# Later transform ends for two batches, the older path for their first tiles, and packed tiles moved to the last four batches

## The chip, the cores and the metric

The kernel runs on one NeuronCore of a Trainium2 chip. The metric is the device time of one execution in microseconds (us), the median of the runs shown. The engines are named as in the profile: PE (TensorE matmuls), PEld (its weight loads), DVE (VectorE), ACT (ScalarE), POOL (GpSimd) and SP (SyncE, which here only issues DMAs).

## The reference, cut to what matters

There are 8 batches of 3008 positions by 256 channels. Each is filtered along the sequence in the frequency domain, and then every position goes through a two-layer network ("MLP") with a sigmoid-gelu between the layers.

```
X = np.fft.rfft(x, axis=1)
y = np.fft.irfft(X * (filt_r + 1j * filt_i)[None], n=3008, axis=1)     # y: (8, 3008, 256)
h = y.reshape(-1, 256) @ w_in                                           # (24064, 2048)
out = (h * (1 / (1 + np.exp(-1.702 * h)))) @ w_out                      # (24064, 256)
```

## The kernel before, in words

**The MLP.** Each batch is cut into 6 tiles `(b, t)`, 48 in all. A tile has 512 positions; the last tile of an even batch has 384. A tile takes 16 chunks `fc` of 128 hidden features. Values are split into a high and a low fp32r part, so one chunk is 12 matmuls: 6 in `first` (L854, into `h`), gelu twice on ACT (L858 and L859), the low part on DVE (L860, `gl`), and 6 in `second` (L879, into `o`). In program order `first` runs two chunks ahead of `second`.

**The transform.** `fft(b)` makes batch b's transform as a prime-factor transform of 64 by 47 points in two stages. It is a generator, and so one "leg" of the plan. For b > 1 the first stage is `packed()` with 24 half steps (butterfly on POOL L524, split L530 and L531, `transform` on PE L542 and then ACT and DVE L544 to L546, result to the DRAM tensor `a_d`). The second stage, `two()`, has 16 rounds. In each, `forward(i)` loads `a_d` (on POOL's queue) and the filter (`load_f`, on SP's queue), transforms (L609, `s`), merges two half results (L628, L629), multiplies by the filter (L631 to L639) and splits the product into `zy` (L643, L644). `backward(i)` transforms back (L609, `i`), merges (L617, L618) and writes `b_d` in DRAM. Batch b's leg runs under the MLP of batch b - 1, and its first stage overlaps the end of the leg before.

**The tiles' last step.** A tile's MLP input `y` is made from `b_d` by one of three paths. `signal`: load `br` (SP), for each half m four fp32 matmuls of 128 columns (L719), a copy on ACT (L727) and a difference on DVE (L728). `turned_signal` with `turned_passes`: load `br`, split on ACT and POOL (L795, L796), 3 matmuls of 512 columns for each half (L308 to L310), a transpose on DVE (L804), a store to the DRAM tensor `z_d`, four loads back, and a split on ACT and POOL (L736, L737). `turned_signal` with `packed_passes` is a variant with 4 matmuls (L769) in place of 6, and with more work on ACT, DVE and POOL (L759, L760, L770, L771, L774, L824). `is_packed` chooses between the last two.

**What sets the order.** The whole program is unrolled. A loop over the "turns" n (one for each chunk; batch b's first tile starts at n = 96 b) emits the MLP, and beside it what falls due: `due` holds for each tile the turns, counted from the chunk 16 before its start, at which its path takes a step, and `steps` holds the legs' steps by a planned time in units of a quarter chunk. `upto` is the planned end of a leg, and `SPACED` places the first stage ahead of the end of the leg before it. The framework's scheduler then orders each engine's instructions by its own estimate, but instructions marked `keep_in_program_order` keep their order among each other on their engine: on PE all matmuls of the legs, the first of each three in `turned_passes`, and the first L719 of `signal` when t is 0. Buffers that matter are the 7 `raw` ones, and the PSUM rings "f" and "h".

Of the kernel before, what the change touches and what calls it, by code (L numbers as in the profile page):

```python
# [14 lines left out]
ALU = mybir.AluOpType  # L15

B, S, D, DFF = 8, 3008, 256, 2048
# [4 lines left out]
Q = 112  # L22
NFC = DFF // P
# [8 lines left out]
def _tables():  # L32
# [66 lines left out]
    e_0 = de[:, 2:4, rows].reshape(P, 2, 2, 2, NH).transpose(0, 1, 4, 3, 2)  # L99
    sign = np.zeros((P, NS))  # L100
    sign[0:48] = sign[64:Q] = _places()[3]
    t1 = t1.reshape(P, 2, 2, NS // 2, 2).transpose(0, 1, 3, 2, 4)
    t1_s = t1[:N1].reshape(N1, 2, P // 2)
# [11 lines left out]
def _places():  # L115

    n1, q = np.arange(N1), np.arange(NH)
    n2 = np.stack([NH - 1 - q, NH + q])  # L120
    at = (N2 * n1[None, :, None] + N1 * n2[:, None, :]) % S
    time = np.where(n2[:, None, :] < N2, at, S)
    p, s = np.arange(48)[:, None], np.arange(NS)[None, :]
    k1 = np.where(s == 0, np.where(p < 24, 0, 32), s)
    k2 = np.where(s == 0, p % 24, p)
    freq = (k1 * N2 * pow(N2, -1, N1) + k2 * N1 * pow(N1, -1, N2)) % S
    sign = np.where(freq > S // 2, -1.0, 1.0)
    freq = np.where(freq > S // 2, S - freq, freq)
    freq = np.where((p < 47) | (s == 0), freq, S // 2 + 1)
    token, odd = [], None  # L130
    for b in range(B):
        for t in range(6):
            if b > 2 or b and t:
                blocks = (b * S + time[:, :, 4 * t : 4 * t + 4]).reshape(4, 32, 4).transpose(0, 2, 1)
                parts = [a.ravel() for a in blocks]
                if t == 5:
                    parts[2:] = parts[2][:96], parts[3][:96]
                    if b % 2:
                        parts[3:] = odd[:32], parts[3], odd[32:]
                    else:  # L140
                        parts[3], odd = parts[3][:32], parts[3][32:]
                token += parts
                continue
            for i in range(4):
                block = b * S + time[:, :, 4 * t + i]
                if 4 * t + i < NH - 1:
                    token.append(block.ravel())
                else:
                    odd = block[0]
    return time, freq, np.concatenate(token), sign  # L150


def _layout(a):

    x, fr, fi, wi, wo = a
    time, freq = _places()[0:2]
    x = np.concatenate([x, np.zeros((B, 1, D), x.dtype)], 1)[:, time]
    x0 = x[:2].reshape(2, P, 6, 4, D).transpose(0, 2, 1, 3, 4)
    x = x[2:].reshape(B - 2, 2, N1, 6, 2, 2, D).transpose(0, 3, 4, 2, 1, 5, 6)
    x = np.concatenate([x0, x.reshape(B - 2, 6, P, 4, D)])  # L160
    f = np.stack([fr, fi], 1)
    f = np.concatenate([f, np.zeros((1, 2, D), f.dtype)])[freq]
    f = f.reshape(48, NS // 2, 2, 2, D).transpose(1, 0, 2, 3, 4)
    f = np.concatenate([f, np.zeros((NS // 2, 16, 2, 2, D), f.dtype)] * 2, 1)
    wi = wi.reshape(2, P, NFC // 2, D).transpose(2, 1, 0, 3)
    wo = wo.reshape(NFC // 2, 2, P, D).transpose(0, 2, 1, 3)
    return {"x": x, "filt": f, "w_in": wi, "w_out": wo}
# [3 lines left out]
def tile_kernel(  # L171
# [9 lines left out]
    nc = tc.nc  # L181
# [38 lines left out]
    table, at = {}, 0  # L220
# [242 lines left out]
    def fft(b):  # L463
# [128 lines left out]
        def load(i):  # L592
            for k in range(2):
                src = a_d[k, 4 * i : 4 * i + 4].rearrange("q n d -> n q d")
                nc.gpsimd.dma_start(zy[0][64 * k : 64 * k + 48, i % 2].rearrange("p k s d -> p (k s) d"), src)  # L595

        def load_f(i):
            for k in range(2):
                load_in(f_buf[64 * k : 64 * k + 48, 2 * (i % 2) : 2 * (i % 2) + 2], fs[i])

        def second(i, m, src, name, k):

            pin = tc.keep_in_program_order
            ps = ring("f", [P, 2, D], f"{name}_{b}_{i}_{k}")
            if i == 0:
                pin(nc.tensor.matmul(ps[:, 0], de_sb[:, k, m + 1], src[:, k, 0], start=True, stop=True))
                nc.tensor.matmul(ps[:, 1], de_sb[:, k, m], src[:, k, 1], start=True, stop=True)
            else:
                pin(nc.tensor.matmul(ps, de_sb[:, k, m], src[:, k], start=True, stop=True))  # L609
            return ps  # L610

        def sides(k):
            return slice(64 * k, 64 * k + 48), slice(64 - 64 * k, 112 - 64 * k)
# [6 lines left out]
        def forward(i):  # L620

            u1, u2 = c_buf[i % 3], u_buf[i % 2]
            fr = f_buf[:Q, 2 * (i % 2) : 2 * (i % 2) + 2]
            f_r, f_i = fr[:, :, 0, :], fr[:, :, 1, :]
            for k in range(2):
                h, o = sides(k)
                ps = second(i, 0, zy[0][:, i % 2], "s2", k)
                nc.scalar.copy(u1[h], ps[o])  # L628
                nc.vector.tensor_tensor(ps[h], ps[h], u1[h], ALU.add)  # L629
                if k:  # L630
                    nc.vector.scalar_tensor_tensor(u2[o], ps[h], -1.0, f_i[h], ALU.mult, ALU.mult)  # L631
                else:
                    nc.vector.tensor_tensor(u2[o], ps[h], f_i[h], ALU.mult)
                nc.vector.tensor_tensor(u1[h], ps[h], f_r[h], ALU.mult)  # L634
                if k == 0:
                    yield
            if i + 2 < 16:
                load(i + 2)
            nc.gpsimd.tensor_tensor(u1, u1, u2, ALU.add)  # L639
            y = zy[0][:, 2 + i % 2]  # L640
            for k in range(2):
                h, o = sides(k)
                nc.scalar.copy(y[h, k], u1[h])  # L643
                nc.gpsimd.tensor_tensor(y[o, k], u1[h], y[h, k].bitcast(F32), ALU.subtract)  # L644
            if i + 2 < 16:
                load_f(i + 2)
            yield
# [18 lines left out]
        return slice(64 * k, 64 * k + 64)  # L666

    def is_packed(b, t):
        return 1 < t < 5 and b > 1 or b == B - 1 and t > 0

    def signal(b, t, y):

# [236 lines left out]
    ys, t2_two, gelu, s1_pool, t2_w, begin = {}, [], [], [], [], []  # L909

    def start(b, t):
        ys[b, t] = sb.tile([P, 2, 2, 512], F32R, tag="y", name=f"y_{b}_{t}")
        return (turned_signal if b > 2 or b and t else signal)(b, t, ys[b, t])

    tus.append(const.tile([P, 4, 2, 2, D], F32, tag="zy", name="w_tu"))
    conv = conversion()
    run(first_fft())
    load_unit(EARLY + 7)
    run(start(0, 0))
    run(conv, 3)  # L920
    load_unit(EARLY + 8)
# [17 lines left out]
    LEAD = 16  # L939

    def width(i):
        return 4 if tiles[i][1] < 5 or tiles[i][0] % 2 else 3

    due = {}
    for j in range(2, len(tiles)):
        b, t = tiles[j]
        if j == 2:
            steps = 23, 26, 27
        else:
            if is_packed(b, t):  # L950
                at = (-8, -4, -3, -2, -1, 0, 1, 2, 4, 8, 9, 10)
            else:
                at = (-6, -2, -1, 0, 1, 3, 9, 10) if b and t else (1, 3, 9) if t else (-1, 2, 3, 4, 5, 7, 11, 12) if b > 2 else (8, 11, 12) if b > 1 else (9, 12, 13)
            steps = [NFC * (j - 1) + k for k in at]
        for n in steps:
            due.setdefault(n, []).append(j)
    steps, passed, since = [], 0, 0
    for b in range(1, B):
        upto = sum(NFC * width(i) for i in range(6 * b)) - 4 * LEAD - ((18 if b > 2 else 12) * width(6 * b - 1) if b > 1 else 26)
        if b == 1:  # L960
            at = np.cumsum(FIRST_LEG) * (upto / sum(FIRST_LEG))
            one, two = at[:12], at[12:]
        else:
            early, beside, alone = SPACED[min(b, 4) - 2]
            first = since - 4 * early
            last = since + 4 * alone
            if not early:
                since = first = first + 4 * 5.5
            lead = first - 4 * np.array([5.0, 4.0, 2.2, 1.1])
            one = [*lead, *(first + (since - first) * np.arange(beside) / max(beside, 1))]  # L970
            one += list(since + (last - since) * (np.arange(24 - beside) / (23 - beside)))
            two = [last + 4 * 1.5, last + 4 * 3, *(last + 4 * 4 + (upto - last - 4 * 4) * np.cumsum([0.0, *LATER[1:]]) / sum(LATER[1:]))]
        one = [*one, two[0]]
        steps += [(when, b, which) for which, ats in enumerate((one, two)) for when in ats]
        since = upto
    steps.sort()
    legs = {}
    for n, (i, fc) in enumerate(turns):
        b, t = tiles[i]
        if n == 0:  # L980
            run(start(*tiles[1]))
# [61 lines left out]
```

## Time and profile before

| | us |
|---|---|
| median of 3 runs (2348.61 to 2349.15) | 2348.69 |
| the profiled execution | 2346.19 |
| its span, first to last instruction | 2344.4 |
| PE busy in it | 2323.5 (99%) |
| DVE, ACT, POOL busy | 1582.4 (67%), 1644.5 (70%), 1191.3 (51%) |

The span is the time from the first to the last instruction of one execution that the hardware profiler took. "Busy" is the time in which an engine had an instruction at work; for PE the ends of matmuls are modelled, so the share alone does not say how near PE is to its best.

### The profile page before, as it was taken

To read this page: it belongs to the slowest core of one execution; us is meant where nothing else is said; L and a number is where in the kernel's file an instruction comes from. 1 tells how busy PE (TensorE), PEld (TensorE's weight loads), DVE (VectorE), ACT (ScalarE), POOL (GpSimd) and SP (SyncE) were. 2 spreads that over 40 slices of the span, in tenths; PEclk is the share of its full clock that TensorE was granted. 3 is DMA by queue.
4 is the path that set the end of the run, shared out by engine and by line. 5 is a ranking of instruction groups with operands and counts; after the bars stand their busy time and mean duration, and the time that the engine had idled before them with its cause. 6 is when DMAs were issued, how large, how long until landed. Compare 5 with 4: busy or idle time off the path is not lost.

```text
span 2344.4 us, 32513 instructions
## 1 busy us (share of the span) xinstructions
PE 2323.5 (99%) x10590; PEld 1937.6 (83%) x10590; DVE 1582.4 (67%) x2374; ACT 1644.5 (70%) x3000; POOL 1191.3 (51%) x1079
## 2 busy tenths in 40 slices
PE   9999999999999999999999999999999999999999
PEld 7878888888888878788888888988888888888887
DVE  7978767677767767577776777667777767533332
ACT  6667768678777767677776777767877777655553
POOL 3035547457556665556655567545764465322220
PEclk9999999999999999999999999999999999999999
DMA  9274545666556565566557575656655565321200
GB/s 338 81 197 104 125 92 160 144 140 144 128 151 130 131 139 151 131 132 130 142 150 151 115 142 136 164 127 140 127 126 151 135 144 110 88 61 48 87 28 19
DMA packets 200120, 301.32 MB, mean 129 GB/s; under 512 B 19216, under 2 KB 136080, under 8 KB 199952
## 3 DMA queue, kind: packets, MB, share of 16 engines
q1 hardware_dynamic: 123248, 188.76, 28.8%
q0 software_dynamic: 46592, 44.05, 13.1%
q10 hardware_dynamic: 30112, 66.44, 11.0%
q8 instruction: 85, 1.39, 0.3%
q14 instruction: 83, 0.68, 0.1%
HBM read 184.35 MB, written 114.82 MB: 128 GB/s over the span
## 4 chain that ended last, share of the span: by engine, by line
PE 62%; DMA 1%; ACT 0%; POOL 0%; issue 0%; DVE 0%; SPq 0%; ACTq 0%; POOLq 0%; DVEq 0%
PE h L854 29%; PE o L879 28%; PE i L609 1%; PE s L609 1%; PE s L542 1%; PE i L769 1%; DMA br<-b_d 0%; PE i L308 0%; PE i L310 0%; PE i L309 0%; DMA z_d<-zt 0%; DMA s_pool<-in_x_dram 0%; SPq L211 0%; DMA a_d<-s_pool 0%; POOL y L737 0%
## 5 line engine op out<-in xcount | busy, mean ns | idle before, releaser
L854 PE MATMUL h<-y,wi 128*128 128x512 f32 (+1 forms) x4608 | 1180.6, 386 | 8.1 <-ACT y L736 3.0
L854 PEld LDWEIGHTS h<-y,wi 128*128 128x128 f32 x4608 | 861.0, 188 | 178.1 <-DVE gl L860 6.3
L860 DVE TENSOR_TENSOR gl<-h,gh 128x512 fp32r<-128x512 f32 (+1 forms) x768 | 518.4, 677 | 528.9 <-ACT h L859 474.3
L879 PE MATMUL o<-gh,wo 128*128 128x512 f32 (+1 forms) x3072 | 836.9, 385 | 0.8 <-ACT gh L858 0.8
L858 ACT ACTIVATE gh<-h 128x512 fp32r<-128x512 f32 (+1 forms) x768 | 452.6, 589 | 419.2 <-PE h L854 345.3
L879 PEld LDWEIGHTS o<-gh,wo 128*128 128x128 f32 x3072 | 573.5, 188 | 111.8 <-ACT gh L858 1.7
L879 PE MATMUL o<-gl,wo 128*128 128x512 f32 (+1 forms) x1536 | 485.4, 385 | 0.4 <-DVE gl L860 0.4
L859 ACT ACTIVATE h<-h 128x512 f32<-128x512 f32 (+1 forms) x768 | 449.3, 585 | 0.1
L879 PEld LDWEIGHTS o<-gl,wo 128*128 128x128 f32 x1536 | 287.3, 188 | 56.4 <-DVE gl L860 1.5
L644 POOL TENSOR_TENSOR zy<-c_buf,zy 48x512 fp32r<-48x512 f32 x224 | 288.5, 1288 | 82.9 <-ACT zy L643 71.3
L639 POOL TENSOR_TENSOR c_buf<-c_buf,u_buf 112x512 f32<-112x512 f32 x112 | 144.7, 1292 | 203.8 <-DVE c_buf L634 202.4
L595 POOL DMA_DIRECT2D zy<-a_d x224 | 130.1, 586 | 220.9 <-PE s L609 126.5
L531 POOL TENSOR_TENSOR e<-s_pool,e 64x512 fp32r<-64x512 f32 x144 | 185.4, 1287 | 50.9 <-ACT e L530 27.9
L618 DVE TENSOR_TENSOR b<-i,b 48x512 f32<-48x512 f32 x224 | 153.7, 686 | 71.6 <-ACT b L617 68.6
L629 DVE TENSOR_TENSOR s<-s,c_buf 48x512 f32<-48x512 f32 x224 | 156.9, 700 | 41.8 <-ACT c_buf L628 35.9
L643 ACT CAST zy<-c_buf 48x512 fp32r<-48x512 f32 x224 | 138.4, 618 | 45.7 <-POOL c_buf L639 39.1
L617 ACT COPY b<-i 48x512 f32<-48x512 f32 x224 | 130.0, 580 | 52.0 <-PE i L609 41.0
L634 DVE TENSOR_TENSOR c_buf<-s,f_buf 48x512 f32<-48x512 f32 x224 | 154.2, 689 | 3.0
L628 ACT COPY c_buf<-s 48x512 f32<-48x512 f32 x224 | 130.1, 581 | 25.0 <-PE s L609 18.3
L524 POOL TENSOR_TENSOR s_pool<-s_pool 128x512 f32<-128x512 f32 x72 | 93.0, 1292 | 82.4 <-DMA s_pool<-in_x_dram 64.8
L545 DVE TENSOR_TENSOR s_pool<-s,s_pool 64x512 f32<-64x512 f32 x144 | 98.8, 686 | 36.2 <-ACT s_pool L544 33.8
L760 POOL TENSOR_TENSOR z<-br,z 64x512 fp32r<-64x512 f32 x80 | 101.7, 1295 | 23.9 <-issue 21.0
(135 smaller groups left out, 1879.3 us busy)
## 6 DMA issues: line engine op xcount, KB each, us to landing
f_buf<-fs SPq DMA_DIRECT2D x224, 192.0 KB, 3.0
zy<-a_d POOLq DMA_DIRECT2D x224, 192.0 KB, 4.0
a_d<-s_pool ACTq DMA_DIRECT2D x144, 256.0 KB, 3.3
br<-b_d SPq DMA_DIRECT2D x124, 256.0 KB, 5.3
out_dram<-out SPq DMA_DIRECT2D x43, 512.0 KB, 3.4
b_d<-b ACTq DMA_DIRECT2D x112, 192.0 KB, 2.5
z_d<-zt SPq DMA_DIRECT2D x40, 512.0 KB, 2.7
s_pool<-in_x_dram SPq DMA_DIRECT2D x36, 512.0 KB, 4.2
```

The source lines that it names most:

```text
L531: nc.gpsimd.tensor_tensor(es[n, h][o], src[t], es[n, h][t].bitcast(F32), ALU.subtract)
L618: nc.vector.tensor_tensor(dst[h], ps[h], dst[h], ALU.add)
L629: nc.vector.tensor_tensor(ps[h], ps[h], u1[h], ALU.add)
L634: nc.vector.tensor_tensor(u1[h], ps[h], f_r[h], ALU.mult)
L639: nc.gpsimd.tensor_tensor(u1, u1, u2, ALU.add)
L643: nc.scalar.copy(y[h, k], u1[h])
L644: nc.gpsimd.tensor_tensor(y[o, k], u1[h], y[h, k].bitcast(F32), ALU.subtract)
L854: ins = nc.tensor.matmul(ps[:, :w], wi_sb[half][:, wk, kc, c], y[:, yk, kc, :w], start=n == 0, stop=n == 5)
L858: nc.scalar.activation(gh[:, :w], ps[:, :w], AF.Gelu_apprx_sigmoid)
L859: gelu.append(nc.scalar.activation(ps[:, :w], ps[:, :w], AF.Gelu_apprx_sigmoid).ins)
L860: nc.vector.tensor_tensor(gl[:, :w], ps[:, :w], gh[:, :w].bitcast(F32), ALU.subtract)
L879: ins = nc.tensor.matmul(pos[m][:, :w], wb[:, P * m : P * m + P], g[:, :w], start=first_one, stop=last_one)
```

## The change

The planned ends of the transforms of batches 3 and 4 (the fourth and the fifth, counted from 0) move from 18 chunks before the batch's first tile to 12 and to 14. The first tiles of these two batches take the path `signal` and its due turns (8, 11, 12) in place of `turned_signal` and (-1, 2, 3, 4, 5, 7, 11, 12); the order of the output positions follows. `is_packed` held for tiles 2 to 4 of batches 2 to 7 and for tiles 1 and 5 of batch 7; now it holds for tiles 1 to 5 of batches 4 to 7. In `forward`, for batch 1 only, the sum of the two halves goes to `u1` in SBUF instead of back into PSUM, the product with `f_r` is one DVE instruction for both halves, and the copies into `zy` run on DVE in place of ACT.

```diff
@@ -130,7 +130,7 @@
     token, odd = [], None
     for b in range(B):
         for t in range(6):
-            if b > 2 or b and t:
+            if b > 4 or b and t:
                 blocks = (b * S + time[:, :, 4 * t : 4 * t + 4]).reshape(4, 32, 4).transpose(0, 2, 1)
                 parts = [a.ravel() for a in blocks]
                 if t == 5:
@@ -626,12 +626,16 @@
                 h, o = sides(k)
                 ps = second(i, 0, zy[0][:, i % 2], "s2", k)
                 nc.scalar.copy(u1[h], ps[o])
-                nc.vector.tensor_tensor(ps[h], ps[h], u1[h], ALU.add)
+                total = ps if b > 1 else u1
+                nc.vector.tensor_tensor(total[h], ps[h], u1[h], ALU.add)
                 if k:
-                    nc.vector.scalar_tensor_tensor(u2[o], ps[h], -1.0, f_i[h], ALU.mult, ALU.mult)
+                    nc.vector.scalar_tensor_tensor(u2[o], total[h], -1.0, f_i[h], ALU.mult, ALU.mult)
                 else:
-                    nc.vector.tensor_tensor(u2[o], ps[h], f_i[h], ALU.mult)
-                nc.vector.tensor_tensor(u1[h], ps[h], f_r[h], ALU.mult)
+                    nc.vector.tensor_tensor(u2[o], total[h], f_i[h], ALU.mult)
+                if b > 1:
+                    nc.vector.tensor_tensor(u1[h], ps[h], f_r[h], ALU.mult)
+                elif k:
+                    nc.vector.tensor_tensor(u1, u1[:Q], f_r, ALU.mult)
                 if k == 0:
                     yield
             if i + 2 < 16:
@@ -640,7 +644,7 @@
             y = zy[0][:, 2 + i % 2]
             for k in range(2):
                 h, o = sides(k)
-                nc.scalar.copy(y[h, k], u1[h])
+                (nc.scalar.copy if b > 1 else nc.vector.tensor_copy)(y[h, k], u1[h])
                 nc.gpsimd.tensor_tensor(y[o, k], u1[h], y[h, k].bitcast(F32), ALU.subtract)
             if i + 2 < 16:
                 load_f(i + 2)
@@ -666,7 +670,7 @@
         return slice(64 * k, 64 * k + 64)
 
     def is_packed(b, t):
-        return 1 < t < 5 and b > 1 or b == B - 1 and t > 0
+        return t > 0 and b > 3
 
     def signal(b, t, y):
 
@@ -910,7 +914,7 @@
 
     def start(b, t):
         ys[b, t] = sb.tile([P, 2, 2, 512], F32R, tag="y", name=f"y_{b}_{t}")
-        return (turned_signal if b > 2 or b and t else signal)(b, t, ys[b, t])
+        return (turned_signal if b > 4 or b and t else signal)(b, t, ys[b, t])
 
     tus.append(const.tile([P, 4, 2, 2, D], F32, tag="zy", name="w_tu"))
     conv = conversion()
@@ -950,13 +954,13 @@
             if is_packed(b, t):
                 at = (-8, -4, -3, -2, -1, 0, 1, 2, 4, 8, 9, 10)
             else:
-                at = (-6, -2, -1, 0, 1, 3, 9, 10) if b and t else (1, 3, 9) if t else (-1, 2, 3, 4, 5, 7, 11, 12) if b > 2 else (8, 11, 12) if b > 1 else (9, 12, 13)
+                at = (-6, -2, -1, 0, 1, 3, 9, 10) if b and t else (1, 3, 9) if t else (-1, 2, 3, 4, 5, 7, 11, 12) if b > 4 else (8, 11, 12) if b > 1 else (9, 12, 13)
             steps = [NFC * (j - 1) + k for k in at]
         for n in steps:
             due.setdefault(n, []).append(j)
     steps, passed, since = [], 0, 0
     for b in range(1, B):
-        upto = sum(NFC * width(i) for i in range(6 * b)) - 4 * LEAD - ((18 if b > 2 else 12) * width(6 * b - 1) if b > 1 else 26)
+        upto = sum(NFC * width(i) for i in range(6 * b)) - 4 * LEAD - ((18 if b > 4 else 14 if b > 3 else 12) * width(6 * b - 1) if b > 1 else 26)
         if b == 1:
             at = np.cumsum(FIRST_LEG) * (upto / sum(FIRST_LEG))
             one, two = at[:12], at[12:]
```

## Rows read from the trace of the kernel before

**Rows 1.** Waits of PE, whole span: us in total, times, longest

```profile
PE h L854 <- ACT y L736: 3.0, 1, 3.0
PE h L854 <- DVE gl L860: 2.8, 4, 1.4
PE s L542 <- DVE s_pool L546: 2.3, 2, 1.4
PE h L854 <- POOL y L737: 2.1, 2, 1.8
PE i L609 <- DVE b L618: 1.9, 2, 1.7
```

**Rows 2.** Windows: length, busy us (instructions) by engine, clock, DMA

```profile
354.40:647.00 292.60, 292.60 (x1305) 242.85 (x1304) 213.75 (x316) 219.06 (x390) 181.11 (x162) 1.00 0.61 144
825.00:852.00 27.00, 24.47 (x104) 19.01 (x103) 15.36 (x24) 18.02 (x32) 16.73 (x16) 1.00 0.70 126
930.00:939.00 9.00, 3.65 (x15) 2.12 (x14) 7.94 (x13) 3.99 (x8) 2.65 (x3) 0.88 0.80 238
...
1180.00:1235.00 55.00, 54.27 (x239) 44.20 (x237) 39.31 (x58) 39.94 (x71) 31.96 (x26) 1.00 0.59 163
...
60.00:157.00 97.00, 96.32 (x438) 78.96 (x437) 88.51 (x150) 63.85 (x119) 20.39 (x13) 1.00 0.40 122
157.00:354.40 197.40, 194.45 (x943) 165.64 (x942) 141.53 (x217) 137.95 (x256) 91.72 (x89) 1.00 0.53 118
```

**Rows 3.** Timeline at batch 3's first tile: start, us, instruction [idle before]

```profile
930.97 2.96 SPq L211 DMA_DIRECT2D y<-z_d  x4
...
938.32 0.62 ACT L736 CAST y<-y 128x512 fp32r<-128x512 f32 x1 [2.55 <-DMA y<-z_d]
...
942.41 5.90 PE L854 MATMUL h<-y,wi 128*128 128x512 f32 x15 [1.77 <-POOL y L737]
```

**Rows 4.** Timeline before 850 us, SP's queue and ACT

```profile
824.15 13.09 SPq L211 DMA_DIRECT2D f_buf<-fs  x2
...
845.75 0.62 ACT L795 CAST bh<-br 128x512 fp32r<-128x512 f32 x1 [1.69 <-DMA br<-b_d]
```

**Rows 5.** Timeline of `signal` at batch 2: its loads, its matmuls

```profile
626.09 2.62 SPq L211 DMA_DIRECT2D br<-b_d  x4
...
641.67 1.05 PE L719 MATMUL i<-tab,br 128*128 128x128 f32 x8
642.48 0.48 PE L854 MATMUL h<-y,wi 128*128 128x512 f32 x1
```

**Rows 6.** L854 alone, windows from a leg's last L609 to the next batch

```profile
621.00:646.90 25.90, 11.56 (x42) 7.89 (x42) 1.00 0.68 179
903.55:938.98 35.43, 12.70 (x60) 10.69 (x60) 0.97 0.67 185
1190.05:1229.90 39.85, 19.42 (x73) 13.67 (x73) 1.00 0.64 177
1473.85:1509.20 35.35, 17.00 (x86) 15.07 (x85) 1.00 0.69 191
```

**Rows 7.** Timeline of POOL at batch 5's first tile

```profile
1508.16 2.54 POOL L737 TENSOR_TENSOR y<-y 128x512 fp32r<-128x512 f32 x2
```

**Rows 8.** Groups by line: xcount, busy us, mean ns, idle before

```profile
L634 DVE TENSOR_TENSOR c_buf<-s,f_buf 48x512 f32<-48x512 f32 x224 | 154.2, 689 | 3.0
...
L643 ACT CAST zy<-c_buf 48x512 fp32r<-48x512 f32 x224 | 138.4, 618 | 45.7 <-POOL c_buf L639 39.1 <-DVE gl L860 2.1 <-DVE b L618 0.7
...
L274 DVE TENSOR_SCALAR w_tu<-w_tu 128x512 uint32<-128x512 uint32 x16 | 6.7, 421 | 0.1
...
L770 ACT COPY uv<-i 64x512 f32<-64x512 f32 x80 | 46.5, 581 | 20.4 <-PE i L769 18.6
...
L760 POOL TENSOR_TENSOR z<-br,z 64x512 fp32r<-64x512 f32 x80 | 101.7, 1295 | 23.9 <-issue 21.0 <-ACT z L759 0.8
...
L281 DVE TENSOR_TENSOR w_tu<-w_tu 128x512 f32<-128x512 f32 x16 | 14.0, 874 | 0.4
```

## The prediction

> **What bounds the kernel now.** I read the page first (PE busy 99% of the span), then the chain of waits, which is PE almost throughout, and so asked only two things: how fast PE goes when nothing stops it, and where it is stopped. In the long window of batch 1, PE issues 1305 matmuls in 292.60 us without idle, 0.224 us each [rows 2]. The waits of PE show how little there is to win elsewhere: the five largest entries sum to 12.1 us [rows 1]. They are not spread out. Placing them by windows, 9.00 - 3.65 = 5.35 us lie between 930 and 939 us [rows 2], and another 1.77 us just after [rows 3]: batch 3's first tile starts late. Two smaller holes are 27.00 - 24.47 = 2.53 us around 847 us and 55.00 - 54.27 = 0.73 us around batch 4's first tile [rows 2].
>
> At batch 3's first tile the chain is plain [rows 3]: SP issues the four loads back from `z_d` over 930.97 to 933.93, ACT's L736 waits for them until 938.32, POOL's L737 follows, and PE's first weights wait for both. After this idle time the next 15 matmuls take 5.90 us, 0.393 each: the granted clock is down to the lower of its two levels (1.2 instead of 2.4 GHz), which cost 5.90 - 15 x 0.224 = 2.5 us. The late start costs 5.35 + 1.77 + 2.5 = 9.6 us in all.
>
> At 847 us an SP instruction is at fault [rows 4]: SP stands on filter loads from 824.15 for 13.09 us, tile 17's `br` load queues behind them, ACT's L795 waits 1.69 us for it with batch 3's L617 behind, and PE's L609 waits 1.7 us for L618 [rows 1].
>
> **How late the legs end.** The plan can be compared with the trace by counting L854 between a leg's last L609 and the next batch's first tile [rows 6]: x42, x60, x73, x86, so 7, 10, 12 and 14 chunks for batches 2 to 5. Working out from `steps` at which turn that L609 is planned, with PE's program three chunks ahead of it, gives 11, 17, 18 and 17. The legs lag by 4, 7, 6 and 3 chunks. From first to last L609 step, the plan gives second stages of 60, 66, 69 and 75 chunks; batch 3's is short, runs beside three packed tiles, and lags most. What the paths need: `turned_signal` at batch 5 takes from 1473.85 [rows 6] to the end of L737 at 1508.16 + 2.54 [rows 7], 36.9 us, and PE just doesn't wait. `signal` at batch 2 has its loads issued by 628.7, 7.7 us after the last L609 [rows 5, 6]. With 4.4 us to land (933.93 to 938.32, the nearest row [rows 3]), 0.81 us of L719 (641.67 to 642.48 [rows 5]), 0.58 + 0.69 us for copy and difference (like L770 and L634 [rows 8]) and some 0.8 us for the second half, it needs 15 us.
>
> **The change part by part.**
>
> *First tiles of batches 3 and 4.* Removed are, for each, a `z_d` store, four loads back on SP, two splits on ACT and POOL before and after, and two transposes. PE: 6 x 0.224 = 1.35 us become 0.81 us, so 2 x 0.54 = 1.1 us are saved for certain. In return the first L719, whose place in PE's order is kept, can stop PE with the MLP behind it, if `br` is late. Batch 3's last L609 is now planned 12 chunks ahead. With a lag of 4 to 7, 5 to 8 chunks of 2.5 to 3.0 us are left, 12 to 24 us against a need of 15. The stall of 9.6 us goes, and 0 to 2.5 us come back; I take 1, since tiles 14 to 16 are no longer packed and the second stage has 71 chunks, so less lag than 7 is due. Batch 4 has 14 - 6 = 8 chunks of 3 us, 24 us: its 0.7 us goes.
>
> *Packing moved.* Six tiles leave (batches 2 and 3), six come (tiles 1 and 5 of batches 4 to 6): PE keeps its 20 packed tiles and gains nothing. A packed tile costs ACT two more casts and four copies, 2 x 0.62 + 4 x 0.58 = 3.6 us, DVE four adds, 2.8 us, and POOL four more instructions of 1.3 us, 5.2 us [rows 8], and two more loads on SP. Under batch 2, where the filter loads block SP, it lifts this load: the 2.5 us at 847 us go (0 to 2.5; I take all, because SP's block begins behind the late rounds of batch 3). It is laid on batches 4 to 6. Batch 5's leg also loses four chunks at its start (75 to 71), so its lag should come near the 6 of batch 4: 1 to 3 chunks of 35.35 / 14.3 = 2.47 us later, against slack that may be as much as 4 us (POOL's L737 stands behind other work there) or none. This is 0 to 7.4 us of new idle at 1509 us, and up to 10 with the clock; I take 2.5.
>
> *Batch 1's `forward`.* ACT loses 32 copies of 0.62 us, 19.8 us. DVE loses two products of 0.69 us a round and gets one, over all partitions but with the same elements each, and two copies from SBUF, not shown in the trace: between 0.42 (L274, one SBUF source) and 0.69 us (a product) [rows 8]. Over 16 rounds DVE gains 16 x (0.15 to 0.69) = 2.4 to 11 us in a window where it is busy 141.53 of 197.40 us and PE idles 2.95 [rows 2]. From 60 to 157 us DVE is busy 88.51 of 97.00 and PE idles 0.68: at 91% it still serves PE. So this is free, 0 with bounds of -2.9 (all idle gone) and +3; the freed PSUM bank helps only where PE waits for one.
>
> DVE's sums and products would now read two SBUF operands (or copy within SBUF) while POOL works in SBUF too. The only such case to price is L281 at 0.874 us against 0.689 for L634 [rows 8]: 0.19 us for each of 16 x 5 instructions, 15 us of DVE, still 85% busy. By the Trainium skill, page "SBUF — State Buffer", section "SBUF: two separate sides", DVE instructions with two SBUF inputs or in a two-port mode and POOL exclude each other for the whole instruction. By that rule the longer L281 is such a wait, and the sum would be rival 4 below instead of 0.
>
> **Sum.** -9.6 - 2.5 - 0.7 - 1.1 + 1.0 + 2.5 = -10.4 us. The profiled execution took 2346.19 (span 2344.4 and 1.8 around it), 2.5 below the median of the runs, 2348.69. So 2335.8 there, and 2338 for the median.
>
> **Rivals.**
>
> 1. *No give-back.* Neither batch 3 nor batch 5 stalls: 2348.7 - 13.9 = 2335; with batch 1's idle gone too, 2332. Against it: batch 5 has no visible slack.
> 2. *The stall moves to batch 5.* Its lag becomes 6 or 7, like batch 3's, with a 384-wide tile ahead of it as there, so 9 to 10 us come back instead of 2.5: 2345. The denser leg and the packed tile 29 speak for it, its 14 chunks against batch 3's 10 against it.
> 3. *The move does nothing at batch 3.* The lag grows with the later end to 9 and more, 3 chunks or 8 us are left of the 15 needed, and 7 us of idle and 2.5 of slow clock stay: 2338 + 8.5 = 2346. Batch 2's leg, denser yet without packed tiles, lags by only 4.
> 4. *Slower, by DVE in batch 1.* Each of the 80 instructions waits for half a POOL instruction of 1.3 us: 52 us, DVE comes to 141.5 + 11 + 52 = 204 us in 197, and PE waits for `gl`. It decides from 91% on (180 us); the 24 us above go to PE: 2362. Against it: only 0.19 us a piece is seen.
>
> **How the numbers follow.** About 0.2%, 4.7 us, is what a measurement of this kernel can tell from no change. Forecast 0.48 (2334 to 2343); rivals 1: 0.14, 2: 0.20, 3: 0.10, 4: 0.08. Below 2344.0 lie the forecast, rival 1, half of rival 2 and a third of rival 3: 0.75. Slower is rival 4, 0.08; the rest, 0.17, is no change. The range of 2331 to 2347 leaves out rival 4 and the ends of 1, 2 and 3, under 0.2.
>
> **What would show it.** Right: no PE wait for L736 or L737 at batch 3's first tile and full clock from 925 to 950 us; no hole near 847; the 40 `z_d` stores (one a turned tile) down to 38; L854 between the last L609 and batch 3's tile some x36 to x48. Wrong: PE waiting for `br` through L719 at batches 3 or 4; a hole with a halved clock around 1500 us; DVE over 90% busy between 157 and 354 us.

## The result, and the profile after

The changed kernel takes 2365.7 us (median of 4 runs, 2363.75 to 2367.21) against 2348.65 (4 runs) for the kernel before: 1.0072 times as long, 95% interval 1.0055 to 1.0089, so about 17 us slower. The forecast was 2338 and faster; even the top of the range, 2347, is passed.

Lines of the changed file stand 4 lower than before from `is_packed` on and in most of `fft`: L858 is the first product (`h`), L862 and L863 gelu, L648 the split into `zy`, L740 and L741 the split into `y`, L773 to L775 the packed products with copy and sum, L828 the packed tile's sums.

How long each batch took, from its first L858 to that of the next (worked out from the traces):

| batch | 1 | 2 | 3 | 4 | 5 | 6 | 7 |
|---|---|---|---|---|---|---|---|
| before, us | 292.6 | 292.0 | 291.0 | 279.4 | 287.9 | 274.3 | 272.9 |
| after, us | 292.6 | 279.1 | 290.8 | 295.8 | 306.9 | 272.6 | 272.5 |

So two things happened that have little to do with each other. Batch 2 won 12.9 us, and batches 4 and 5 lost 16.4 and 19.0. Inside them the tiles that grow most are (5,4), 48.3 to 64.3 us, and (4,5), 39.2 to 48.5 us. They are not alike. Windows over tile (4,5), before and then after (length, busy us and instructions by engine, granted clock, DMA):

```profile
1470.18:1509.34 39.16, 39.16 (x215) 37.65 (x214) 29.36 (x47) 30.56 (x62) 21.09 (x17) 1.00 0.66 180
```
```profile
1464.96:1513.49 48.53, 45.13 (x233) 40.15 (x231) 36.72 (x58) 37.81 (x75) 30.69 (x26) 1.00 0.62 170
```

Of its 9.3 us PE idles only 48.53 - 45.13 = 3.4; the rest is work that comes later than before, 233 matmuls in place of 215. Tile (5,4) is a real stop, as shown below.

The gain first. Windows of the profile after:

```profile
825.00:852.00 27.00, 27.00 (x120) 22.36 (x120) 20.12 (x30) 21.23 (x38) 17.56 (x16) 1.00 0.44 99
...
930.00:939.00 9.00, 9.00 (x43) 7.56 (x42) 5.60 (x9) 7.05 (x13) 3.62 (x3) 1.00 0.59 152
```

The hole at 847 us and the late start of batch 3, 24.47 and 3.65 us busy in [rows 2], are full, and the clock is whole. L858 alone, in the windows from the last L609 of a leg to batches 3, 4 and 5:

```profile
901.44:926.87 25.43, 12.09 (x60) 10.91 (x61) 1.00 0.60 151
1182.55:1217.68 35.13, 17.50 (x67) 12.39 (x66) 1.00 0.63 169
1481.87:1513.49 31.62, 12.56 (x61) 10.74 (x61) 1.00 0.70 193
```

x60, x67 and x61, so 10, 11 and 10 chunks against the 10, 12 and 14 of [rows 6].

The loss. Waits of PE in the profile after (us in total, times, longest):

```profile
PE i L609 <- POOL zy L648: 9.6, 2, 9.0
PE o L883 <- ACT gh L862: 5.9, 8, 2.1
PE s L606 <- DMA zy<-a_d: 2.4, 3, 1.1
PE h L858 <- DVE gl L864: 2.3, 5, 0.8
PE s L609 <- DMA zy<-a_d: 1.9, 1, 1.9
```

The waits of [rows 1] for L736 and L737, now L740 and L741, are gone from the head of the list (0.6 us each is left, at batch 5's first tile); one wait of 9.0 us at a leg's L609 stands in their place. Its surroundings in the timeline, PE, then POOL (start, us, instruction, idle before):

```profile
1761.09 0.47 PE L609 MATMUL i<-zy,de_sb 128*128 128x512 f32 x1 [0.61 <-DVE c_buf L636]
1770.58 0.80 PE L609 MATMUL i<-zy,de_sb 128*128 128x512 f32 x1 [9.02 <-POOL zy L648]
1771.91 0.79 PE L609 MATMUL i<-zy,de_sb 128*128 128x512 f32 x1 [0.54 <-POOL zy L648]
...
1756.54 2.54 POOL L828 TENSOR_TENSOR yf<-uvt 128x512 f32<-128x512 f32 x2
1761.58 1.27 POOL L524 TENSOR_TENSOR s_pool<-s_pool 128x512 f32<-128x512 f32 x1 [2.50 <-PE i L609]
1762.80 1.28 POOL L643 TENSOR_TENSOR c_buf<-c_buf,u_buf 112x512 f32<-112x512 f32 x1
1764.15 1.26 POOL L531 TENSOR_TENSOR e<-s_pool,e 64x512 fp32r<-64x512 f32 x1
1765.49 1.26 POOL L741 TENSOR_TENSOR y<-yf,y 128x512 fp32r<-128x512 f32 x1
1766.71 1.26 POOL L524 TENSOR_TENSOR s_pool<-s_pool 128x512 f32<-128x512 f32 x1
1767.93 1.26 POOL L741 TENSOR_TENSOR y<-yf,y 128x512 fp32r<-128x512 f32 x1
1769.27 2.59 POOL L648 TENSOR_TENSOR zy<-c_buf,zy 48x512 fp32r<-48x512 f32 x2
```

The last round of batch 6's leg needs L648, and POOL runs it behind the six others listed from 1761.58 on, among them the two L741 that make `y` of tile (5,5). That tile's MLP is what PE runs next, so both are late at the same time. Windows around it:

```profile
1759.00:1772.00 13.00, 2.84 (x10) 1.47 (x8) 5.16 (x8) 5.83 (x10) 10.13 (x10) 0.68 0.39 123
1772.00:1785.00 13.00, 13.00 (x46) 10.46 (x47) 9.12 (x14) 8.19 (x15) 1.96 (x5) 0.80 0.49 112
```

10.2 us of idle, and a granted clock of 0.80 of full after it (13 x 0.20 = 2.6 us lost), make 12.8 of the 16.0 us by which tile (5,4) is longer.

A smaller stop lies where the prediction looked for one, at batch 5's first tile, where L858 waits for L740 and then for L741:

```profile
1505.00:1520.00 15.00, 12.71 (x47) 9.54 (x46) 10.65 (x17) 9.80 (x19) 14.35 (x12) 0.81 0.82 244
```

That is 2.3 us of idle and 15 x 0.19 = 2.9 us by the clock, some 5 us.

Why is tile (5,5) late? Its steps in the profile after: products and splits by line (x count: least, median, largest ns; first and last start in us), and two issues on SP:

```profile
L773 PE MATMUL i<-z,t_w x4: 389/390/390, 1726.3 to 1739.5; 128*128 128x512 f32 x4
```
```profile
L764 POOL TENSOR_TENSOR z<-br,z x4: 1288/1294/1314, 1707.9 to 1717.0; 64x512 fp32r<-64x512 f32 x4
```
```profile
1742.78 0.34 SPq L211 DMA_DIRECT2D z_d<-zt  x1
1747.32 2.78 SPq L211 DMA_DIRECT2D uvt<-z_d  x4
```

The inputs of the four products are ready at 1717.0 + 1.3 = 1718.3, yet PE issues them over 1726.3 to 1739.5, and does not idle between 1718.3 and the last of them: it does other work first. Store, loads, sums and `y` follow from there. Three theories could explain this: the packed path has too much work for POOL or ACT beside a leg; its steps meet the leg's last ones in the wrong order or start too late; or it is held up by something shared that is no engine.

### The profile page after: what moved, and what is told of

Its sections match the earlier page's. It is cut to its first block, busy times and chain, and to the rows that moved or that the text cites. A ratio compares the mean times of both kernels' runs of the same rounds, so it can differ in the third digit from the quotient of the medians.

```text
span 2365.4 us, 32457 instructions
## 1 busy us (share of the span) xinstructions
PE 2333.4 (99%) x10610; PEld 1941.4 (82%) x10610; DVE 1591.1 (67%) x2390; ACT 1622.5 (69%) x2964; POOL 1185.2 (50%) x1071
## 5 line engine op out<-in xcount | busy, mean ns | idle before, releaser
L858 PE MATMUL h<-y,wi 128*128 128x512 f32 (+1 forms) x4608 | 1189.6, 387 | 3.7 <-DVE gl L864 2.3
L858 PEld LDWEIGHTS h<-y,wi 128*128 128x128 f32 x4608 | 862.6, 189 | 175.0 <-DVE gl L864 7.5
L862 ACT ACTIVATE gh<-h 128x512 fp32r<-128x512 f32 (+1 forms) x768 | 452.4, 589 | 441.6 <-PE h L858 375.3
L863 ACT ACTIVATE h<-h 128x512 f32<-128x512 f32 (+1 forms) x768 | 449.3, 585 | 0.1
L648 POOL TENSOR_TENSOR zy<-c_buf,zy 48x512 fp32r<-48x512 f32 x224 | 292.4, 1305 | 84.3 <-ACT zy L647 64.3
L630 DVE TENSOR_TENSOR s<-s,c_buf 48x512 f32<-48x512 f32 x192 | 134.4, 700 | 46.3 <-ACT c_buf L628 41.7
L647 ACT CAST zy<-c_buf 48x512 fp32r<-48x512 f32 x192 | 118.7, 618 | 43.8 <-POOL c_buf L643 40.5
L636 DVE TENSOR_TENSOR c_buf<-s,f_buf 48x512 f32<-48x512 f32 x192 | 132.1, 688 | 2.6
L764 POOL TENSOR_TENSOR z<-br,z 64x512 fp32r<-64x512 f32 x80 | 101.6, 1292 | 21.9 <-issue 18.5
```

Of the source, the lines that this page charges most:

```text
L630: nc.vector.tensor_tensor(total[h], ps[h], u1[h], ALU.add)
L858: ins = nc.tensor.matmul(ps[:, :w], wi_sb[half][:, wk, kc, c], y[:, yk, kc, :w], start=n == 0, stop=n == 5)
L862: nc.scalar.activation(gh[:, :w], ps[:, :w], AF.Gelu_apprx_sigmoid)
L863: gelu.append(nc.scalar.activation(ps[:, :w], ps[:, :w], AF.Gelu_apprx_sigmoid).ins)
```

## The experiments

A difference in us below is the distance between two ratios times 2348.65. By that the kernel after stands at +16.9 us. (The expectations on record reckon with differences of medians, which come out up to 2 us larger.)

**Which part loses.** `e1_packing_back` is the kernel after with `is_packed` of before; `e2_packing_alone` the kernel before with the new one; `e4_plan_alone` the kernel before with the new ends of legs and first tiles only.

```diff
-        return t > 0 and b > 3
+        return 1 < t < 5 and b > 1 or b == B - 1 and t > 0
```

> The changed kernel with is_packed as before; plan, first tiles and forward as changed. Theory A (tile 5 of batches 4 and 5, packed beside the last rounds of the next leg, stands ahead of those rounds on POOL and stops PE) and theory B (all the packing moved to batches 4 to 6 is too much for ACT and POOL): the 35 us lost under batches 4 and 5 go, 2330 to 2337. Theory C (leg 5, which starts later and has 71 chunks for its second stage in place of 75, is the cause): the loss stays, 2350 or more, though batch 3's gain of 10 stays too.

> The kernel before with only is_packed changed. Theories A and B: tiles (4, 5) and (5, 4) take 9 and 16 us more as they do after, and the 2.5 us at 847 us go, so 2365 to 2375. Theory C: no loss under batches 4 and 5, 2344 to 2349.

> The kernel before with only the planned ends and the first tiles of batches 3 and 4 changed (packing and forward as before). By the prediction's terms without packing: 9.6 us at batch 3's first tile, 2.5 or less at 847 us since those tiles are packed again, 0.7 at batch 4, 1.1 for PE: 2334 to 2338. If forward in batch 1 has a part in the gain of the run with the packing put back: 2340 or more.

They gave 2335.3 us, 0.995 [0.9933, 0.9967]; 2377.52 us, 1.0133 [1.0118, 1.0148]; and 2335.23 us, 0.9952 [0.9935, 0.9968]. So theory C, the denser leg 5, is out; e2 lies 2.5 us above its range, with the sign that theories A and B gave it. The plan is worth 11.3 us by itself; the packing costs 31.2 us alone and 16.9 + 11.7 = 28.6 on top of the plan. With the plan alone the hole at 847 us is gone as well (27.00 us busy in 825 to 852 us). With the packing alone batch 2 also shortens, to 282.2 us: either part takes most of the late start of batch 3 away, and only one can have it. The two versions without the new packing are the fastest of all here, and better than both kernels. What the packing costs is idle time and clock: in the profiled executions PE is busy 2333.4 of 2365.4 us after and 2321.3 of 2334.4 in e1, so it idles 32.0 against 13.1 us, and the mean granted clock is 0.995 against 1.000. That is 18.9 us and 2365.4 x 0.005 = 11.8 us of the 31.0 us between these two executions.

`e11_forward_back`: the kernel after with batch 1's `forward` of before.

```diff
-                total = ps if b > 1 else u1
+                total = ps
...
-                (nc.scalar.copy if b > 1 else nc.vector.tensor_copy)(y[h, k], u1[h])
+                nc.scalar.copy(y[h, k], u1[h])
```

> The changed kernel with batch 1's forward as before. Batch 0 takes 1.3 us less (it took 294.4 before and 295.7 after): 2364. If DVE in batch 1 were a cause of the loss (the slower rival of the prediction), 2350 or less.

2361.89 us, 1.0063 [1.0048, 1.0078], which overlaps with after. This part is not the cause.

**Which tiles.** `e5_no_tile5` leaves tile 5 of batches 4 to 6 on the older path, `e9_one_tile` only tile (5,5), and `e10_mid_b4` tiles 1 and 5 of these batches.

```diff
-        return t > 0 and b > 3
+        return 0 < t < 5 and b > 3 or b == B - 1 and t > 0   # e5
+        return t > 0 and b > 3 and (b, t) != (5, 5)          # e9
+        return 1 < t < 5 and b > 3 or b == B - 1 and t > 0   # e10
```

> The changed kernel, but tile 5 of batches 4 to 6 not packed (tile 1 is). Theory A: tiles (4, 5) and (5, 4) come back to 39 and 48 us, 2336 to 2343. Theory B: only the share of these three of six tiles goes, about 2350. Theory C: no change, 2362 to 2367.

> The changed kernel with only tile (5, 5) not packed. If this one tile's POOL work (L828, L741), which stands between the sum L643 and the split L648 of leg 6's last round in POOL's fixed order, makes the 16 us, tile (5, 4) takes 48 us again and the time is 2349 to 2351. If the load of all the packed tiles makes it, most of the loss stays: 2358 or more.

> The changed kernel with tiles 2 to 4 of batches 4 to 6 packed and tiles 1 and 5 not (batch 7 as changed), so batches 2 and 3 have no packed tile and PE 24 matmuls more than in the run with the packing put back, about 5 us. If tile 1 makes what is left of the loss (12.9 us between the run without tile 5 and the run with the packing put back): 2335 to 2341. If the missing packed tiles of batches 2 and 3 make it: 2346 to 2349.

2348.17 us, 1.0007 [0.9998, 1.0016]; 2350.9 us, 1.0015 [1.0005, 1.0025]; 2337.31 us, 0.996 [0.9945, 0.9975]. The first missed the range of theory A and is nearer to B's 2350; the other two lie in the ranges for one tile and for tile 1, and with (5,5) unpacked tile (5,4) takes 48.0 us again. So tile 5 of three batches costs 15.3 us, of which one tile, (5,5), has 13.4; tile 1 costs 1.6 + 9.4 = 11.0; and leaving batches 2 and 3 unpacked costs 2.3 (e10 against e1).

**Not the amount of work.** A packed tile puts more on POOL and ACT. `f1_sums_on_dve` moves L828 of tiles 1 and 5 from POOL to DVE, `f2_pool_relief` L764 too, `f4_pool_relief_all` both for all packed tiles of batches 4 to 6, and `f3_act_relief` moves L774 of tiles 1 and 5 from ACT to DVE.

```diff
-                ins = nc.gpsimd.tensor_tensor(yj[:, :, j], uv[:, :, 0], uv[:, :, 1], ALU.subtract if j else ALU.add)
+                ins = (nc.vector if t in (1, 5) and b < 7 else nc.gpsimd).tensor_tensor(yj[:, :, j], uv[:, :, 0], uv[:, :, 1], ALU.subtract if j else ALU.add)
```

> The changed kernel, same tiles packed; in tiles 1 and 5 of batches 4 to 6 the two sums of L828 run on DVE in place of POOL: 2.6 us less on POOL and 1.4 more on DVE in each of six tiles. If the packed tiles' POOL work is what makes POOL late (and PE behind it), a part of the 30 us goes: 2345 to 2358. If ACT's casts and copies of the packed tiles are the cause: 2362 to 2368. If DVE is: over 2366.

> As the run before, and the four differences L764 of the same six tiles on DVE too: 7.8 us less on POOL in each (packing had added 5.2), 4.2 more on DVE. POOL as the cause: nearly all of the loss goes, 2335 to 2345. ACT as the cause: 2362 to 2368. DVE as the cause: 2370 or more.

> The changed kernel, same tiles packed; in tiles 1 and 5 of batches 4 to 6 the four copies of L774 run on DVE in place of ACT: 2.3 us less on ACT, 2.8 more on DVE in each. POOL as the cause: 2360 to 2367. ACT as the cause: 2345 to 2358. DVE as the cause: 2368 or more.

> As the second of these runs, but in all 15 packed tiles of batches 4 to 6. POOL as the cause: 2332 to 2342, and batches 4 and 5 at 279 and 288 us or less. DVE as the next bound (it gets 4.2 us more in each tile, at 71 to 78% busy before): slower than the second run by 3 or more.

2365.42 us, 1.0078 [1.0063, 1.0093]; 2366.94, 1.0098 [1.008, 1.0115]; 2360.36, 1.0063 [1.0048, 1.0078]; 2371.18, 1.0109 [1.0094, 1.0124]. None helps by more than the intervals allow, and f4 harms. By the ranges f1 and f2 speak for ACT and f3 for POOL, so they agree on no engine. In f1 the four products of (5,5) start where they did; in f2, where their inputs come from DVE and the last starts at 1714.0 in place of 1717.0, they are no earlier. First f1, then f2:

```profile
L773 PE MATMUL i<-z,t_w x4: 389/389/389, 1726.6 to 1739.8; 128*128 128x512 f32 x4
```
```profile
L773 PE MATMUL i<-z,t_w x4: 389/389/389, 1728.1 to 1741.7; 128*128 128x512 f32 x4
```

**Not the order of the last steps, not a late start.** `e8_tile5_later` puts the last three steps of tile 5 three chunks later, behind the leg's last round; `g1_tile5_earlier` puts all its steps four chunks earlier; `g5_legs_end_earlier` ends legs 5 to 7 four chunks earlier.

```diff
-                at = (-8, -4, -3, -2, -1, 0, 1, 2, 4, 8, 9, 10)
+                at = (-8, -4, -3, -2, -1, 0, 1, 2, 4, 11, 12, 13)   # e8, tile 5
+                at = (-12, -8, -7, -6, -5, -4, -3, -2, 0, 4, 5, 6)  # g1, tile 5
...
-        upto = ... - ((18 if b > 4 else 14 if b > 3 else 12) ...
+        upto = ... - ((22 if b > 4 else 14 if b > 3 else 12) ...    # g5
```

> The changed kernel, all tiles packed as in it, but the last three steps of tile 5 of batches 4 to 6 (the sums L828 and the two splits L741) fall due three chunks later (11, 12, 13 for 8, 9, 10). If their place ahead of the last round on POOL is the cause, the hole at 1761 us closes at an unchanged amount of work: 2350 to 2356. If the amount of work is the cause: 2362 to 2367.

> The kernel after with all twelve steps of the packed tile 5 of batches 4 to 6 due four chunks earlier. Theory A, the path is simply started too late for its own length: the tile's sums come before the leg's last rounds, and the cost of packing tile 5 (about 17 us) goes: about 2348 us. Theory B, the path is held up on its way by what it shares with the leg (the ring of three PSUM banks), so that an earlier start meets the tile before it instead: under 6 us is won, 2360 us or more, and tile (5,4) or (4,4) or (4,5) still shows several us of PE idle.

> The kernel after with the legs of batches 5 to 7 planned to end 22 chunks ahead of their batch in place of 18, so that the last rounds lie four chunks ahead of the packed tile 5's sums. Theory C, the loss needs the leg's last round and tile 5's sums to be late in the same place: the stall in (5,4) goes, 10 to 16 us won, 2350 to 2356 us. Theory B: the legs are denser by 4 chunks of about 90, and the ring is later still: no gain, 2362 us or more.

All three are slower than after: 2386.74 us, 1.0175 [1.016, 1.019]; 2384.19, 1.0153 [1.0138, 1.0168]; 2377.5, 1.0127 [1.0112, 1.0142]. g1 and g5 fall where theory B put them; e8 falls in neither of its ranges. In e8, PE waits for the other one of the two late things, the last piece of `y` itself:

```profile
PE h L858 <- POOL y L838: 8.7, 1, 8.7
```

An earlier start (g1) loses 19.0 us more. That hints at something full on the way, which the next runs tried.

**The ring of PSUM banks.** The legs' L609 and L542 and the tiles' products write to PSUM by turns from the ring "f", three banks. A packed tile takes four turns of it, the path that it replaces two. `g3_h_banks` lets the products of tiles 1 and 5 of batches 4 to 6 take turns of the MLP's ring "h", also three banks; `g6_h_banks_all` those of tiles 1 to 5. `g4_four_banks` leaves the shared bank with "f" from batch 1 on: four and two.

```diff
-                ps, h, o = ring("f", [P, 2, D], ...
+                ps, h, o = ring("h" if t in (1, 5) and b < B - 1 else "f", [P, 2, D], ...   # g3
+                ps, h, o = ring("h" if b < B - 1 else "f", [P, 2, D], ...                   # g6
...
         if n == 6 * NFC:
-            shared[0] = "h"
+            shared[0] = "f"                                                             # g4
```

> The kernel after with the four products of the packed tiles 1 and 5 of batches 4 to 6 put into the MLP's ring of PSUM banks in place of the ring of three that the legs use. Theory B, the legs' ring is what runs late (a packed tile takes four turns of it, the older path two): the products stand within 4 chunks of their due turn in place of 7 to 9, and 15 us or more of the 30 are won: 2350 us or less. Theory A (too late a start): the products are a little earlier, under 8 us won. It may lose some us at the MLP's own banks under both.

> The kernel after with the fourth, shared PSUM bank left with the legs' ring in place of the MLP's for the whole of the program, so four banks and two. Theory B: the products of tile (5,5) stand within 5 chunks of their due turn and the stalls in tiles (5,4) and (4,5) go, a gain of 15 to 30 us less what the MLP loses with two banks (not known; a chunk then has one bank less ahead, between 0 and tens of us). Theory A: the stalls at (5,4) and (4,5) stay, 16 and 9 us.

> The kernel after with the products of all packed tiles of batches 4 to 6, 1 to 5, in the MLP's ring of PSUM banks. If the legs' ring is the whole of the loss, what is left of it with tiles 1 and 5 alone moved (13.6 us: tile (5,4) at 60.4 us, (4,4) at 53.4) goes as well, since tiles 2 to 4 then take no turns of it either: 2335 to 2340 us. If the rest is another limit (the last sums on POOL beside the leg's last rounds), tile (5,4) stays near 60 us and the time between 2345 and 2352 us.

2349.29 us, 1.0005 [0.9996, 1.0015]; 2363.41, 1.0063 [1.0048, 1.0078]; 2344.58, 0.9989 [0.998, 0.9998]. g4 is not to be told from after; g3 gives back 15.7 us and g6 19.5, with the same instructions on every engine and only another bank under the products. g6 lies between its two ranges, with 53.9 us for tile (5,4), neither the 48 of before nor near 60. Splits and products of tile (5,5) in g6:

```profile
L764 POOL TENSOR_TENSOR z<-br,z x4: 1285/1292/1298, 1693.7 to 1700.4; 64x512 fp32r<-64x512 f32 x4
```
```profile
L773 PE MATMUL i<-z,t_w x4: 389/389/389, 1699.2 to 1710.3; 128*128 128x512 f32 x4
```

Here the products go over 1699.2 to 1710.3 and the splits end at 1701.7. How far the last product of a tile stands behind the turn at which it is due, in chunks (L858 or L854 begun by then, in groups of six, less that turn, less one; 2.0 is a product that stands where the program puts it):

| tile | before | e1 | after | e2 | g1 | g3 | g4 | g6 |
|---|---|---|---|---|---|---|---|---|
| (4,2) | 5.0 | 5.0 | 6.0 | 5.0 | 6.0 | 3.8 | 2.0 | 2.0 |
| (4,5) | | | 7.2 | 5.5 | 2.5 | 2.0 | 2.0 | 2.0 |
| (5,2) | 4.0 | 4.0 | 6.0 | 8.0 | 8.0 | 4.0 | 2.0 | 2.0 |
| (5,4) | 5.2 | 5.2 | 5.7 | 10.7 | 10.7 | 5.0 | 2.0 | 2.0 |
| (5,5) | | | 8.7 | 10.0 | 8.3 | 2.0 | 3.0 | 2.0 |

With the ring of three every tile lags, and a lag of 4 to 5 costs nothing: before and e1 have it in these batches, with no such stop. In the kernel after it goes up to 7.2 and 8.7 in the fifth packed tile; in e2 and g1, the two slowest kernels of the table, it grows from tile to tile up to 10.7. In f1 to f4 (5,5) lags by 8.7, 8.2, 9.0 and 8.8, so shifting work did not move it. With one more bank (g4), or off that ring (g6), it is 2.0 in nearly every tile. In g4 batches 4 and 5 win 8.9 and 8.3 us on after, but batches 1 to 3 lose 9.3, 2.1 and 2.7, since the MLP has a bank less:

```profile
PE h L858 <- DVE gl L864: 9.9, 14, 1.8
```

`g7_back_and_h_banks` asks what the loan of the MLP's ring costs: e1, with the products of its 15 packed tiles of batches 2 to 6 in "h" (g6 has 15 there too). It is not the same set of tiles, so it prices the loan only roughly.

> The kernel after with the tiles packed that before packs (2 to 4 of batches 2 to 6, 1 to 5 of batch 7), and their products, batch 7's apart, in the MLP's ring. With packing as before alone it took 2335.3 us, with 8.3 us of PE idle in all. If turns of the legs' ring still cost anything there, it is at most those 8 us: 2331 to 2335 us; if not, 2335 to 2338 us by what the MLP's ring loses.

2342.88 us, 0.9983 [0.9974, 0.9993], above both ranges: 7.7 us slower than e1, with PE's longest entry again L858 waiting for `gl`. g6 is 9.1 us from e1. If the loan costs g6 the same 7.7, which wasn't measured by itself, some 1.4 of the 28.6 us are left for anything else.

A packed tile also takes five of the turns of the seven `raw` buffers where the older path takes two. No run changes that by itself. g6 leaves those turns as they are and its products are on time, so they are not what made the products late.

## Why the prediction was wrong, point by point

- **Late start of batch 3's first tile (-9.6) and the hole at 847 us (-2.5): right.** Batch 2 is 12.9 us shorter. Ten chunks were left behind the leg, in place of the 5 to 8 reckoned, so the lag was 2 and not 4 to 7, and x60 stands for the forecast x36 to x48; PE never waits for the path `signal` (the +1.0 is 0). The 2.5 us were put down to the packing that leaves batch 2; e4, which leaves it there, wins them too. That reason was wrong, the sum was not.
- **Batch 4's first tile (-0.7) and the transposes (-1.1):** nothing contradicts them; the 38 stores to `z_d` forecast are there. The plan as a whole, -13.9 without a give-back, came to -11.3 (e4).
- **Batch 1's `forward` (0): right.** The batch takes 292.6 us as before. DVE's groups by line in the profile after (mean ns behind the bar):

```profile
L647 DVE CAST zy<-c_buf 48x512 fp32r<-48x512 f32 x32 | 15.3, 478 | 2.8 <-POOL c_buf L643 2.2
L634 DVE TENSOR_TENSOR u_buf<-c_buf,f_buf 48x512 f32<-48x512 f32 x16 | 13.3, 833 | 0.5
L638 DVE TENSOR_TENSOR c_buf<-c_buf,f_buf 112x512 f32<-112x512 f32 x16 | 11.8, 736 | 0.2
```

  A copy is 478 ns, inside the bounds of 0.42 and 0.69 us; DVE is busy 148.97 us between 157 and 354.4 us against 141.53 in [rows 2], 7.4 more, inside 2.4 to 11. The L634 that reads two SBUF operands takes 833 ns against 684 for the same product with one operand in PSUM (L633 in the profile before), 0.15 us longer, where rival 4 had half a POOL instruction, 0.65. By the Trainium skill, page "SBUF — State Buffer", section "SBUF: two separate sides", such an instruction and POOL's exclude each other; the direction agrees, the price here is small, with POOL busy 96.31 of those 197.4 us.
- **Packing moved (+2.5, bounds 0 to 7.4, 10 with the clock): this is the step that failed.** It was priced as so many instructions on ACT, DVE and POOL, on the ground that PE "keeps its 20 packed tiles and gains nothing", and the give-back was looked for at one place, batch 5's first tile. It measures 28.6 us. At batch 5's first tile it is some 5 us, inside the bounds; the largest part is at tile (5,4), which neither the sum nor a rival names. Five packed tiles in a row beside a leg take 20 turns of the legs' ring, where three packed and two older ones took 16. The engines' busy times say nothing of that, and runs that shift the busy time (f1 to f4) don't either. The prediction thought of a PSUM bank only where "PE waits for one", and PE does not wait for these. Rival 2 was right for a part: batch 5's leg lags by 7 (17 chunks planned, 10 left), and the hole with a lower clock near 1500 us is there. But it had 9 to 10 us in all and nothing at (5,4).
- **Batch 5's leg four chunks denser:** no cause. e1 has the same denser leg and no such stall; batch 5 takes 288.0 us there.

What is shown: moving the products to other banks takes away their lag and 19.5 us. What is only argued: how the ring holds them. When the chip runs, the banks stand empty. In the profile after, PE and then DVE:

```profile
1726.32 0.39 PE L773 MATMUL i<-z,t_w 128*128 128x512 f32 x1
1728.13 0.39 PE L773 MATMUL i<-z,t_w 128*128 128x512 f32 x1
...
1731.99 0.39 PE L609 MATMUL i<-zy,de_sb 128*128 128x512 f32 x1
...
1733.35 0.39 PE L773 MATMUL i<-z,t_w 128*128 128x512 f32 x1
...
1734.93 0.39 PE L609 MATMUL i<-zy,de_sb 128*128 128x512 f32 x1
...
1738.11 0.39 PE L542 MATMUL s<-e,t_two 128*128 128x512 f32 x1
...
1739.47 0.39 PE L773 MATMUL i<-z,t_w 128*128 128x512 f32 x1
...
1728.33 0.67 DVE L775 TENSOR_TENSOR uv<-i,uv 64x512 f32<-64x512 f32 x1
```

By the plan the ring's turns come here in the order L773, L773, L609, L773, L609, L542, L773, and PE runs them in that order. So, three turns on, the L773 at 1733.35 takes the bank of the one at 1726.32, which DVE had read out by 1729.00, 4.4 us before. So PE doesn't wait for the bank when it runs; the product stands where it does in PE's order, which was fixed when the program was built. That the ring's turns were the limit then, so that each further turn was put one more place back, fits g3, g4 and g6, but no run shows the builder's reasons. The Trainium skill, page "Perfetto Trace Analysis", section "Matmuls", says that independent groups of matmuls should go round different banks, so that the reading of one overlaps with the next; g4 agrees in the direction for batches 4 and 5 (8.9 and 8.3 us won), though here the banks were already empty when PE came to them, and it shows that the bank must come from somewhere.

Left open is why batch 6, with five packed tiles and a leg beside them, doesn't fall behind: its tile (6,5) lags by 3.8 chunks in the kernel after and no tile is longer than before. The same count for the legs' own L609 gives a hint. At the first L609 of round 14 (of 0 to 15) leg 6, which runs under batch 5, lags by 8.8 chunks in the kernel after, 7.0 in e1, 2.0 in g4 and 1.0 in g6; leg 7, which runs under batch 6, by 3.0 in the kernel after. The plan gives leg 7's second stage 75 chunks and leg 6's 69. That the tighter leg is needed for the loss was not tested.

## What to carry to other kernels

Count what a variant takes of each shared, rotating buffer, PSUM banks first, and not only its instructions on each engine: the packed path was level on PE and took twice the turns. Where a small step moves far behind its inputs while its engine is never idle, look at what it must take turns for; an earlier start can then make it worse, as in g1. And when a change has parts, time each alone: here the plan gave 11.3 us and the packing took 28.6.

## What the runs showed that was not expected

- A step can stand late without a wait on the chip, and moving it to other banks (g6) put it on time: the bank was empty for 4.4 us, the product's inputs were ready 8 to 21 us before it (1718.3 against 1726.3 to 1739.5), and PE had other work in front and did not idle in between.
- After 9.02 us without a matmul, broken only by one short one before, PE's granted clock was 0.80 on average over the next 13 us, so for part of them at the lower of its two levels (1.2 and not 2.4 GHz), and the first matmul took 0.80 us where the same line took 0.47 ahead of the wait.
